# Order of the first loads: one whole x chunk on SP, the first wk piece and the gate vector first on ACT's queue

## The chip, the cores and the metric

The kernel runs on one core of a Trainium2 chip. A core has five engines that run beside one another: TensorE (PE, matrix products; PEld is its loading of stationary operands), VectorE (DVE), ScalarE (ACT), GpSimd (POOL) and SyncE (SP). Data comes from HBM by DMA. In this kernel DMAs are issued from SP and from ACT, each with a queue of its own, and run on the core's 16 DMA engines. The metric is the device time of one execution in microseconds; less is better.

## The reference, cut to what matters

```python
x = A_x                                              # 2048 rows x 640, bf16
g = _sigmoid((x * gate_w).sum(-1, keepdims=True))    # gate_w: 640 values
a = _A_ref(x, A_wqkv, A_wo)    # linear attention, 32 heads of 20: phi(q) (phi(k)^T v) / den, then @ wo
b = _B_ref(x, B_w1, B_w2, B_w3, B_w4)   # gelu(LN(x) @ w1), shifted rows, @ w2, + x; then an MLP 640-1728-640
return g * a + (1 - g) * b
# phi(t) = (t + 1 where t > 0, else exp(t)) + 1e-6
```

The first thing that the kernel computes is `phi(x @ wk)`, where `wk` is the middle third of `wqkv`, and with it the gate's logit `x @ gate_w`.

## The kernel before, in words

The 2048 rows are 16 chunks of 128 (`NCH`); the 640 columns are 5 pieces of 128 (`DC`). TensorE needs x with its columns on the partitions, so there is a tile `xT` of 5 pieces by 2048 rows. The order of instructions on each engine is the order of the code (a manual schedule).

Loads. `x_sb` chunk 0 comes as two halves of 64 rows, one first on SP's queue and one first on ACT's (L126, L127). Then come the five pieces of `wk` (`load_wk`, L124): piece 1 and 3 on SP, 0, 2 and 4 on ACT. The gate vector (`g5`, five rows of 128 values, 1.2 KB, L130) is third on ACT, behind wk piece 0. Then SP issues seven transposing DMAs that load chunks 1 to 15 straight into `xT` (`load_xT`, L121), and the loads of all later stages, among them wq (L136) and the other x chunks (`load_x`, L118). A DMA gets one of eight completion semaphores in turn, so the issue of a later one waits until the DMA that last used its semaphore has landed: before, the second transposing DMA waits for an x half, the third for wk piece 0, the fourth for wk piece 1, the fifth for the gate vector.

The opening on TensorE. `warmup(n, w)` (L201 to L203) issues `n` products of constants, `w` columns wide, whose results nobody reads. The program opens with `warmup(6)` (512 columns) and `warmup(3, P)` (128 columns) on L205 and L206. Then chunk 0 is transposed on TensorE in two turns (L212): pieces 0 and 1, then 2 to 4; VectorE copies each turn into `xT` (L213). Between the turns the gate vector is transposed (L215), and VectorE copies it into a further column of `wk_sb` (L216), so that the second product of each wk piece also gives the logit. Three more narrow fillers follow (L217; the first of them waits for that copy, since it writes the same PSUM tile).

Then the k stage (`k_mm`, L191): for each chunk and each piece two products, of 320 and 321 columns. In chunk 0 one filler of 256 columns stands behind each of the first four pieces (L221). ACT copies the logit of each finished chunk (`ylog`, L195) and takes the exponential (L183), VectorE makes `phi` from it. After 16 chunks come the q products (L233), and all later stages follow on TensorE without a pause: kv (L308), w1 (L342), w2 (L414), attention (L445), w3 (L461) and w4 (L480).

Of the kernel before, what the change touches and what calls it, by code (L numbers as in the profile page):

```python
# [16 lines left out]
def kernel(  # L17
# [14 lines left out]
    P = 128  # L32
    S, D = A_x.shape[1], A_x.shape[2]
# [21 lines left out]
    x2 = A_x.rearrange("b s d -> (b s) d")  # L55
# [13 lines left out]
    def pair():  # L69
        return ps.tile([P, 2, 512], F32, name="pp")  # L70


    x_sb = const.tile([P, NCH, D + 2], BF16)
# [41 lines left out]
    sp, aq, gq = nc.sync, nc.scalar, nc.gpsimd  # L115

    def load_x(c0, c1):
        sp.dma_start(x_sb[:, c0:c1, 0:D], x2[c0 * P:c1 * P, :].rearrange("(c p) d -> p c d", p=P))  # L118
# [4 lines left out]
    def load_wk(q, dc):  # L123
        q.dma_start(wk_sb[:, dc, 0:D], A_wqkv[dc * P:(dc + 1) * P, D:2 * D])  # L124

    for q, r0 in ((sp, 0), (aq, P // 2)):  # L126
        q.dma_start(x_sb[r0:r0 + P // 2, 0, 0:D], x2[r0:r0 + P // 2, :])  # L127
    load_wk(sp, 1)
    load_wk(aq, 0)
    aq.dma_start(g5[:], gate_w.rearrange("(c p) -> c p", p=P))  # L130
    load_wk(aq, 2)
    load_wk(sp, 3)
# [68 lines left out]
    def warmup(n, w=TS):  # L201
        for i in range(n):
            nc.tensor.matmul(warm[:, 1, 0:w], lhsT=one[:, 0:P], rhs=one[:, 0:w], start=True, stop=True)  # L203

    warmup(6)  # L205
    warmup(3, P)  # L206
    kp = pair()
    turns = [(pair()[:, 0, :].bitcast(BF16), a, b) for a, b in ((0, 2), (2, DC))]
    tg = warm[:, 0, :].bitcast(BF16)
# [387 lines left out]
```

## Time and profile before

| what | us |
|---|---|
| median of 3 runs | 270.51 |
| the runs | 270.07, 270.51, 271.04 |
| the profiled execution (the third of these) | 271.04 |
| its span on the core | 269.3 |
| TensorE busy | 262.1 |
| start of the first product (a filler) | 0.83 |
| start of the gate vector's transpose | 6.76 |
| start of the first k product | 7.49 |
| end of the k stage | 32.42 |

Times inside an execution are counted from the start of the span. A line of the timeline gives the start, the duration, the engine, the line of the kernel, the operation, what it writes and reads, and in brackets the idle time of the engine ahead of it with what ended that. A small q behind an engine's name is its queue, which issues DMAs and waits. A line of the waits has who waited for whom, then the total, the number of times and the longest. A line of DMA issues ends with the median time from issue to landing.

### The profile page before, as it was taken

How to read it: one execution, taken by the hardware profiler on the slowest of the kernel's cores; microseconds unless marked ns; L12 is line 12 of the kernel's file. 1: busy time of each engine (PE TensorE's matmuls, PEld its weight loads, DVE VectorE, ACT ScalarE, POOL GpSimd, SP SyncE). 2: the span in 40 equal slices, each digit the busy share in tenths (PEclk: the TensorE clock that was granted, in tenths of full speed). 3: DMA queues.
4: the chain of work that ended last, by engine and by line, in shares of the span. 5: the costliest groups of instructions: out<-in, count | busy, mean ns of one | idle time of the engine just before them, and what ended most of it. 6: DMA issues, size and time to landing. Idle time of an engine off the chain costs nothing.

```text
span 269.3 us, 4258 instructions
## 1 busy us (share of the span) xinstructions
PE 262.1 (97%) x1744; PEld 163.6 (61%) x1744; DVE 139.4 (52%) x270; ACT 85.1 (32%) x126; POOL 20.1 (7%) x55
## 2 busy tenths in 40 slices
PE   4999999999999999999999999999999999999994
PEld 1677655588855564565576555576555576555763
DVE  0278868799967498866323256233256233112132
ACT  1155544421244815831322131332131332142100
POOL 7100010002320032001000000100000100000000
PEclk9999999999999999999999999999999999999999
DMA  6999988004657524900041100041100041100011
GB/s 146 187 194 361 373 261 323 0 7 88 124 108 91 77 49 80 332 6 0 2 97 51 49 0 2 0 95 53 49 0 2 0 96 54 49 0 2 0 49 49
DMA packets 46108, 23.61 MB, mean 88 GB/s; under 512 B 35466, under 2 KB 45450, under 8 KB 46090
## 3 DMA queue, kind: packets, MB, share of 16 engines
q1 hardware_dynamic: 45568, 22.78, 32.9%
q10 hardware_dynamic: 522, 0.57, 1.2%
q8 instruction: 13, 0.21, 0.3%
q14 instruction: 5, 0.04, 0.1%
HBM read 12.21 MB, written 2.62 MB: 55 GB/s over the span
## 4 chain that ended last, share of the span: by engine, by line
PE 95%; DMA 2%; ACT 1%; ACTq 1%; DVE 0%; issue 0%
PE pp L480 21%; PE pp L461 21%; PE pp L191 9%; PE pp L308 8%; PE pp L414 8%; PE pp L445 8%; PE pp L342 8%; PE pp L233 8%; DMA g<-in_gate_w_dram 2%; PE pp L469 1%; PE pp L489 1%; ACT m_sb L382 1%; PE pp L361 1%; PE pp L248 0%; PE pp L203 0%; ACTq L124 0%
## 5 line engine op out<-in xcount | busy, mean ns | idle before, releaser
L461 PE MATMUL pp<-lnxT,w_sb 128*128 128x512 bf16 x260 | 60.4, 379 | 0.0
L480 PE MATMUL pp<-w_sb,h 128*128 128x256 bf16 (+1 forms) x416 | 57.9, 299 | 0.0
L463 ACT ACTIVATE h<-pp 128x1024 bf16<-128x1024 f32 (+1 forms) x28 | 26.9, 961 | 82.2 <-PE pp L461 82.2
L480 PEld LDWEIGHTS <-h 128*128 128x128 bf16 x416 | 40.3, 98 | 16.6 <-issue 1.1
L461 PEld LDWEIGHTS <-w_sb 128*128 128x128 bf16 x260 | 25.4, 98 | 26.8
L496 DVE SCALAR_TENSOR_TENSOR oc<-pp,omg,x 128x640 bf16<-128x640 f32 x15 | 12.9, 882 | 44.0 <-ACT h2x L472 21.3
L448 DVE SCALAR_TENSOR_TENSOR x<-pp,gate,x 128x640 f32<-128x640 f32 x16 | 13.9, 867 | 29.4 <-PE pp L445 29.4
L191 PE MATMUL pp<-wk_sb,xT 128*128 128x320 bf16 (+1 forms) x160 | 24.9, 317 | 0.0
L417 DVE TENSOR_TENSOR x<-pp,x_sb 128x640 f32<-128x640 f32 x16 | 13.1, 820 | 22.6 <-PE pp L414 22.6
L183 ACT ACTIVATE e<-pp 128x640 bf16<-128x640 f32 (+1 forms) x26 | 21.5, 826 | 9.6 <-PE pp L233 9.6
L445 PE MATMUL pp<-m_sb,pqT 128*128 128x320 bf16 x160 | 24.3, 299 | 0.0
L414 PE MATMUL pp<-w_sb,hsT 128*128 128x320 bf16 x160 | 23.9, 299 | 0.1
L308 PE MATMUL pp<-x_sb,pk 128*128 128x320 bf16 (+1 forms) x160 | 22.3, 300 | 0.0
L233 PE MATMUL pp<-xT,hsT 128*128 128x512 bf16 x100 | 21.7, 379 | 0.0
L308 PEld LDWEIGHTS <-pk 128*128 128x128 bf16 x160 | 18.8, 117 | 3.5
L191 PEld LDWEIGHTS <-xT 128*128 128x128 bf16 x160 | 16.5, 104 | 7.1
L414 PEld LDWEIGHTS <-hsT 128*128 128x128 bf16 x160 | 15.6, 98 | 8.2 <-issue 0.2
L445 PEld LDWEIGHTS <-pqT 128*128 128x128 bf16 x160 | 15.7, 98 | 7.7
L342 PE MATMUL pp<-lnxT,w_sb 128*128 128x512 bf16 x80 | 17.9, 379 | 0.0
L233 PEld LDWEIGHTS <-hsT 128*128 128x128 bf16 x100 | 11.8, 118 | 9.7
L278 POOL TENSOR_SCALAR rstd<-mv 128x4 f32<-128x4 f32 (+1 forms) x11 | 3.4, 312 | 160.1 <-DVE mv L284 160.1
L184 DVE TENSOR_SCALAR e<-e 128x640 bf16<-128x640 bf16 (+1 forms) x26 | 9.5, 365 | 10.5 <-ACT e L183 9.0
(77 smaller groups left out, 196.4 us busy)
## 6 DMA issues: line engine op xcount, KB each, us to landing
out_dram<-oc SPq DMA_DIRECT2D x15, 160.0 KB, 1.8
w_sb<-in_B_w_dram SPq DMA_DIRECT2D x1, 2160.0 KB, 8.5
w_sb<-in_B_w_dram SPq DMA_DIRECT2D x1, 2080.0 KB, 10.0
x_sb<-in_A_x_dram SPq DMA_DIRECT2D x2, 640.0 KB, 9.4
x_sb<-in_A_x_dram SPq DMA_DIRECT2D x1, 1120.0 KB, 8.1
wo_sb<-in_A_wo_dram SPq DMA_DIRECT2D x6, 160.0 KB, 7.4
hsT<-in_A_wqkv_dram SPq DMA_DIRECT2D x1, 800.0 KB, 5.6
m_sb<-in_A_wqkv_dram SPq DMA_DIRECT2D x1, 800.0 KB, 11.1
```

Source lines behind the costliest of these rows:

```text
L183: nc.scalar.activation(ev, src, ACT.Exp)
L191: nc.tensor.matmul(pt[:, hf, 0:n], lhsT=xT[:, dc, c * P:(c + 1) * P], rhs=wk_sb[:, dc, hf * HD:hf * HD + n], start=(dc == 0), stop=(dc == ...
L233: nc.tensor.matmul(pt[:, t % 2, :], lhsT=wq_sb[:, dc, :].rearrange("p (m j) -> p j m", j=DC)[:, j], rhs=xT[:, dc, t * TS:(t + 1) * TS], st ...
L308: nc.tensor.matmul(pt[:, hf, 0:HD + hf], lhsT=w, rhs=x_sb[:, c, hf * HD:(hf + 1) * HD + hf], start=(c == 0), stop=(c == NCH - 1))
L342: nc.tensor.matmul(pt[:, i, :], lhsT=w, rhs=lnxT[t][:, dc, :], start=(dc == 0), stop=(dc == DC - 1))
L414: nc.tensor.matmul(pt[:, hf, 0:HD], lhsT=hsT[:, fc, 2 + c * P:2 + (c + 1) * P], rhs=w2_sb[:, fc, hf * HD:(hf + 1) * HD], start=(fc == 0), ...
L417: nc.vector.tensor_tensor(x1[:].rearrange("p (h e) -> p h e", h=2), pt[:, :, 0:HD], x_sb[:, c, 0:D].rearrange("p (h e) -> p h e", h=2), op ...
L445: nc.tensor.matmul(pt[:, hf, 0:HD], lhsT=pqT[:, j, c * P:(c + 1) * P], rhs=m_sb[:, j, hf * HD:(hf + 1) * HD], start=(j == 0), stop=(j == D ...
L448: nc.vector.scalar_tensor_tensor(x1, pt[:, :, 0:HD], gate[:, c:c + 1], x1, op0=ALU.mult, op1=ALU.add)
L461: nc.tensor.matmul(pt[:, k, :], lhsT=w3_sb[:, dc, fc * P:(fc + 1) * P], rhs=lnT[:, dc, :], start=(dc == 0), stop=(dc == DC - 1))
L463: nc.scalar.activation(h2[:, 2 * i * TS:(2 * i + n) * TS], pt[:].rearrange("p h e -> p (h e)")[:, 0:n * TS], ACT.Gelu_apprx_tanh)
L480: nc.tensor.matmul(dst, lhsT=st[t]["h2"][:, fc * TS + cc * P:fc * TS + (cc + 1) * P], rhs=w4_sb[:, fc, a:b], start=start and fc == 0, stop ...
```

## The change

The first x chunk is loaded by one DMA on SP's queue. On ACT's queue wk piece 0 is now first and the gate vector second; pieces 2 and 4 follow as before. SP still issues wk pieces 1 and 3 second and third. There is one DMA less in all, so the semaphores are handed out differently: the second transposing DMA now waits for wk piece 0, the third for the x chunk, the fourth for the gate vector, the fifth for wk piece 1. In the opening of TensorE there are seven wide fillers and one narrow, in place of six and three. Nothing else differs; the lines below move up by one.

```diff
-    for q, r0 in ((sp, 0), (aq, P // 2)):
-        q.dma_start(x_sb[r0:r0 + P // 2, 0, 0:D], x2[r0:r0 + P // 2, :])
+    load_x(0, 1)
+    load_wk(aq, 0)
     load_wk(sp, 1)
-    load_wk(aq, 0)
     aq.dma_start(g5[:], gate_w.rearrange("(c p) -> c p", p=P))
     load_wk(aq, 2)
     load_wk(sp, 3)
     load_wk(aq, 4)
...
-    warmup(6)
-    warmup(3, P)
+    warmup(7)
+    warmup(1, P)
```

## The prediction

> **What bounds the kernel now.** I read the page first, then the waits and the chain of the opening, its timeline, and the DMA landings.
>
> The page: the profiled execution took 271.04 us, its span is 269.3, so 1.7 lie around the span. It is the slowest of the three runs, 0.53 above the median of 270.51. "Within 0.3%" below means within 0.81 us of that median.
>
> ```profile
> span 269.3 us, 4258 instructions
> PE 262.1 (97%) x1744; PEld 163.6 (61%) x1744; DVE 139.4 (52%) x270; ACT 85.1 (32%) x126; POOL 20.1 (7%) x55
> ```
>
> TensorE is busy for 97% of the span. The waits of the first 14 us and the waits of TensorE from there on say where the rest is:
>
> ```profile
> PE pp L215 <- DMA g<-in_gate_w_dram: 2.7, 1, 2.7
> PE pp L203 <- PEq L581: 0.8, 1, 0.8
> ```
>
> Apart from its first instruction, TensorE waits once in the whole program, 2.7 us for the 1.2 KB gate vector. After it the products follow one another to the end. So what starts that stream earlier shortens the kernel by as much, unless another wait comes in. The opening in order of time (ACT's queue and TensorE):
>
> ```profile
> 0.79 0.56 ACTq L127 DMA_DIRECT2D x_sb<-in_A_x_dram  x1
> 0.83 3.04 PE L203 MATMUL pp<-const-bfloat16-1.0 128*128 128x512 bf16 x9 [0.83 <-PEq L581]
> 1.39 0.86 ACTq L124 DMA_DIRECT2D wk_sb<-in_A_wqkv_dram  x1
> 2.27 0.58 ACTq L130 DMA_DIRECT2D g<-in_gate_w_dram  x1
> ...
> 3.66 0.42 PE L212 MATMUL pp<-ident,x_sb 128*128 128x128 bf16 x2
> 6.76 0.18 PE L215 MATMUL pp<-ident,g 5*128 5x5 bf16 x1 [2.68 <-DMA g<-in_gate_w_dram]
> ...
> 7.49 0.74 PE L191 MATMUL pp<-wk_sb,xT 128*128 128x320 bf16 x2
> ```
>
> The gate vector is issued third on ACT's queue, at 2.27, and lands 4.4 later, at 6.7. The pace comes next. The chain gives 0.53 for a pair of L191 products, while chunk 0 is worked; ACT's copy of each finished chunk's gate logit shows the pace behind it:
>
> ```profile
> 7.69 0.53 PE pp L191 x2
> ```
> ```profile
> 11.26 0.16 ACT L195 COPY ylog<-pp 128x1 f32<-128x1 f32 x1 [6.09 <-PE pp L191]
> 13.38 0.16 ACT L195 COPY ylog<-pp 128x1 f32<-128x1 f32 x1 [1.36 <-PE pp L191]
> 14.74 0.16 ACT L195 COPY ylog<-pp 128x1 f32<-128x1 f32 x1 [0.60 <-PE pp L191]
> ```
>
> Chunk 1 takes 2.12, chunk 2 and all later ones 1.36, half of 5 x 0.53. TensorE goes over to the double pace inside chunk 1, at (2.12-1.36)/(2.65-1.36) = 59% of its slow products: 11.02 (where chunk 1 begins) + 1.56, about 12.6. That is 5.9 us after its last idle ended at 6.76. The 3.0 us of fillers from 0.83, ended by the wait, were not enough for it. (The granted clock reads full throughout; the pace is what I go by.)
>
> Last, the DMA views of 2.0 to 4.1 us, then of 4.1 to 6.7 (q1 is SP's queue, q10 ACT's; packets, MB, share), and the DMAs issued near 3.0 with their time to landing:
>
> ```profile
> DMA packets 482, 0.54 MB, mean 259 GB/s; under 512 B 58, under 2 KB 482, under 8 KB 482
> q10 hardware_dynamic: 203, 0.23, 36.8%
> ```
> ```profile
> DMA packets 812, 0.43 MB, mean 166 GB/s; under 512 B 582, under 2 KB 812, under 8 KB 812
> q10 hardware_dynamic: 183, 0.20, 55.3%
> q1 hardware_dynamic: 629, 0.23, 48.7%
> ```
> ```profile
> wk_sb<-in_A_wqkv_dram ACTq DMA_DIRECT2D x1, 160.0 KB, 5.6
> xT<-in_A_x_dram SPq DMA_TRANSPOSE x1, 6.6
> ```
>
> From 4.1 on the packets are small ones of the transposing DMAs, and less is moved.
>
> **The change part by part.**
>
> *Fillers.* Before x's turn 6 wide and 3 narrow products become 7 and 1. The weight loads of wide ones start 0.43 apart, three narrow ones take 0.32: +0.43 - 0.21 = 0.22. The first x transpose moves from 3.66 to 3.88. Today this hides in the 2.68 of wait for the vector; if that cover is gone it costs 0.22.
>
> *First x chunk in one DMA on SP.* The halves land 2.3 and 2.6 after 0.79, at 3.1 and 3.4. The whole chunk is 80 KB more on SP's queue, while the first wk piece now runs beside it from ACT. Bounds: 3.1 (SP's half) and 4.2 (SP's second DMA, issued at 1.40, landing 2.8 later, after 240 KB). I take the middle, 3.7, ahead of the fillers' end; the upper bound costs 0.3. SP still issues three DMAs before its first transposing DMA (2.49), so those keep their times; POOL's queue issues none. The third transposing DMA waits on the semaphore of wk piece 0 for 0.7 now (SP's waits); the order after gives it x's semaphore, and the second gets that of piece 0.
>
> The Trainium skill, "DMA: Bandwidth & Descriptors", Queues, rings and completion order, says that each DMA engine goes round between the queues that have work, packet by packet; this speaks against the change, since x then shares the engines with wk piece 0, where its halves shared them with each other only. By that rule x lands with 320 KB moved instead of 160; the rows' bound of 4.2 has 240 KB moved on SP alone and about as much beside it, so rule and bound ask for no other sum.
>
> *Gate vector.* One issue of 0.56 goes from in front of it: issued near 1.7. Ahead of it on ACT's queue stand 160 KB, not 240. Queue 10 (ACT's) moves 0.23 MB in 2.0 to 4.1, which is all that stood ahead of the vector; at this 0.11 MB/us 160 KB take 1.5, so its turn comes near 3.6 instead of 4.1. It landed 2.6 after its turn, in that second stretch of 166 GB/s. Bounds: 3.6 + 0.3 = 3.9 (the two x halves landed 0.3 apart) and 3.6 + 2.6 = 6.2. I take 4.2, because its turn now lies in the stretch in which x and wk piece 1 landed without such a delay. Then the first k product comes 0.73 later (6.76 to 7.49 today), at 4.9 for 7.49. VectorE's copies of x's transposes (0.29, 0.36) end before they are needed.
>
> *What is late next.* The five wk pieces are needed 0.75 apart (L191 pair and filler): 4.9, 5.7, 6.4, 7.2, 7.9. Before, pieces 0, 1 and 3 landed at 5.8, 4.2, 7.1; 0 is now first on its queue, so in time. Pieces 2 and 4 landed at 2.88 + 5.6 = 8.5 and 9.0, and the second x chunk (2.49 + 6.6) at 9.1. Pieces 2 and 4 have 80 KB less ahead of them. Queue 10 moves 0.20 MB in 4.1 to 6.7, so they gain between 0 and 1.05: piece 2 lands between 7.4 and 8.5. I take 7.5: the queue is never empty in that stretch, so less ahead shows nearly in full. From it chunk 0 has 2 x 0.75 + 0.53 at the slow pace: chunk 1 starts at 9.5; at the fast pace it waits for its x at 9.1. Bounds for chunk 1's start: 9.1 and 10.5, before 11.02.
>
> *Pace.* TensorE now works without a hole from 0.83 to 6.4: 5.6 us, where 5.9 preceded the change of pace. If that is enough, chunk 1 runs at 1.36 and its extra 0.76 goes too; if the pace changes at 12.6 as before, half of what is won in the start is lost again.
>
> The Trainium skill, "TensorE: Matmul & The Clock Gate", Part 1, has the clock released after a busy window of about 3.4 us, free-running. By it the opening's 5.6 us hold a whole window in (5.6-3.4)/3.4, about 6 of 10 phases; the trace's one change of pace fits such a window and does not prove it.
>
> *Sum.* Chunk 1 starts at 9.4 instead of 11.02: -1.62. No slow products in it: -0.76. Together -2.38: 271.04 - 2.4 = **268.7**. I make no deduction for the profiled run's 0.53 above the median: I estimate that this is when the pace changes, and in this case all of chunk 1 is fast. Later stages take it: x chunks 8 to 11 land at 10.69 + 6.9 = 17.6 and are then needed at 9.4 + 7 x 1.36 = 18.9.
>
> **The rivals.**
>
> *B, early start, old pace.* The vector lands in time, but the waits for wk piece 2 break the run and the pace changes near 12.6. Won: (11.02 - 9.5)/2 = 0.76: 270.3. For it: 5.6 is under 5.9. Against: the run is near that length.
>
> *C, the vector still late.* It keeps its 2.6 of delay and lands at 6.2 instead of 6.7. Half of 0.6 is won at the old pace: 270.7. For it: its delay has nothing to do with its size. Against: its turn comes before the transposing DMAs.
>
> *D, slower: the second x chunk becomes the wait.* SP's queue holds 80 KB more ahead of its transposing DMA. Queue 1 moves 0.23 MB in 4.1 to 6.7, so 80 KB can cost 0.9: it lands at 10.0 and TensorE idles until then. If the 5.9 us to the fast pace count from there, the slow stretch costs 5.9/2 = 2.95 instead of 0.76: (10.0 - 11.02) + 2.95 - 0.76 = +1.2: 272.2. It decides for slower (over 271.3) from a landing of 9.1 on, with TensorE still slow by then. For it: it landed at 9.1 before. Against: ACT's queue, which shares the engines, has 80 KB less.
>
> **How the numbers follow.** A 0.45, B 0.22, C 0.13, D 0.20. A's own range is 267.9 (chunk 1 at 8.9) to 269.5 (at 10.2). Without D the range is 267.9 to 271.3. Faster: nearly all of A and a quarter of B (270.3 less the spread of 0.5) = 0.50; the same: the rest of B and C = 0.28; slower: D and a little of C = 0.22.
>
> **What would show it.** L215 near 4.2 with an idle under 0.3 before it (over 1.5: C). First L191 near 4.9; idle of TensorE before the third pair, put down to a wk piece on ACT's queue; chunk 1 from 9.4. The first two logit copies 1.36 apart, for A; about 2.6 for B and D. TensorE waiting on xT past 9.1 would be D. The step likeliest to fail is the pace, then piece 2's landing.

## The result, and the profile after

The changed kernel takes 266.87 us (median of 4 runs, 266.47 to 266.91) against 270.76 for the kernel before on the same chip (4 runs): a ratio of 0.9857, with a 95% interval of 0.9834 to 0.9879. It is faster by 3.9 us. The prediction had 268.7 with a range of 267.9 to 271.3, so the direction is right and the time lies 1.0 us below the range.

The page of the profiled execution after (266.86 us):

```profile
span 265.2 us, 4253 instructions
PE 260.5 (98%) x1743; PEld 162.8 (61%) x1743; DVE 139.3 (53%) x270; ACT 85.1 (32%) x126; POOL 20.3 (8%) x55
```

The waits of the first 14 us, and ACT's queue and TensorE in order of time. All kernel lines have a number one lower than before: L190 are the k products, L211 the transposes of x, L214 that of the gate vector.

```profile
PE pp L202 <- PEq L580: 0.8, 1, 0.8
PEld L211 <- DMA x_sb<-in_A_x_dram: 0.3, 1, 0.3
```
```profile
0.79 0.40 ACTq L124 DMA_DIRECT2D wk_sb<-in_A_wqkv_dram  x1
1.22 0.59 ACTq L129 DMA_DIRECT2D g<-in_gate_w_dram  x1
1.85 0.84 ACTq L124 DMA_DIRECT2D wk_sb<-in_A_wqkv_dram  x2
```
```profile
3.88 0.42 PE L211 MATMUL pp<-ident,x_sb 128*128 128x128 bf16 x2
4.23 0.18 PE L214 MATMUL pp<-ident,g 5*128 5x5 bf16 x1
...
5.04 0.74 PE L190 MATMUL pp<-wk_sb,xT 128*128 128x320 bf16 x2
5.57 0.42 PE L202 MATMUL pp<-const-bfloat16-1.0 128*128 128x256 bf16 x1
5.79 0.74 PE L190 MATMUL pp<-wk_sb,xT 128*128 128x320 bf16 x2
6.32 0.34 PE L202 MATMUL pp<-const-bfloat16-1.0 128*128 128x256 bf16 x1
6.50 0.44 PE L190 MATMUL pp<-wk_sb,xT 128*128 128x320 bf16 x2
...
7.26 6.98 PE L190 MATMUL pp<-wk_sb,xT 128*128 128x320 bf16 x50
```

The vector's transpose starts at 4.23 instead of 6.76, and no wait takes its place: from 3.88 on TensorE does not wait. The k products go from 0.74 for a pair to 0.44 between 5.79 and 6.50, so the fast pace is there within chunk 0. ACT's logit copies show the same:

```profile
7.73 0.16 ACT L194 COPY ylog<-pp 128x1 f32<-128x1 f32 x1 [3.73 <-PE pp L190]
9.09 0.16 ACT L194 COPY ylog<-pp 128x1 f32<-128x1 f32 x1 [0.60 <-PE pp L190]
```

The k stage ends at 28.13 instead of 32.42, 4.29 earlier. The first k product comes 2.45 earlier (7.49 to 5.04), chunk 0 takes 2.49 instead of 3.53 (1.04), and chunk 1 takes 1.36 instead of 2.16 (0.80). The rest of the program is as long as before: TensorE's last product ends 233.3 after the k stage in both. The three parts make 4.29 together.

What the prediction did not have is the loads. Here is the DMA view of 4.1 to 6.7 after, then the issues near 2.2 (after; wk piece 4 and the second x chunk), with the time to landing:

```profile
DMA packets 1191, 0.59 MB, mean 226 GB/s; under 512 B 896, under 2 KB 1191, under 8 KB 1191
...
q1 hardware_dynamic: 923, 0.29, 67.8%
q10 hardware_dynamic: 268, 0.30, 39.7%
```
```profile
wk_sb<-in_A_wqkv_dram ACTq DMA_DIRECT2D x1, 160.0 KB, 4.5
xT<-in_A_x_dram SPq DMA_TRANSPOSE x1, 5.1
```

In the same stretch as before 226 GB/s are moved instead of 166. ACT's queue, which moves wk pieces there, needs less of the engines for more bytes: 268 packets for 39.7% of 16 engines over 2.6 us are 62 ns a packet, where 183 for 55.3% were 126 ns. So the loads on ACT's queue and the second x chunk land 1.8 to 2.5 us earlier (the vector by its transpose; times in us from the start of the span). On SP's queue wk piece 1 lands at 4.1 as before, piece 3 at 6.1 for 7.1, and the first x chunk a little later, at 3.6 for 3.1 and 3.4:

| run | wk 0 | vector's transpose | wk 2 | wk 4 | second x chunk | chunk 1 starts |
|---|---|---|---|---|---|---|
| before | 5.8 | 6.76 | 8.5 | 9.0 | 9.1 | 11.02 |
| after | 3.8 | 4.23 | 6.3 | 6.7 | 7.3 | 7.53 |

### The profile page after: what moved, and what is told of

It reads as the page before. It is cut to its first block, busy times and chain, and to the rows that moved or that the text cites. A ratio compares the mean times of both kernels' runs of the same rounds, so it can differ in the third digit from the quotient of the medians.

```text
span 265.2 us, 4253 instructions
## 1 busy us (share of the span) xinstructions
PE 260.5 (98%) x1743; PEld 162.8 (61%) x1743; DVE 139.3 (53%) x270; ACT 85.1 (32%) x126; POOL 20.3 (8%) x55
## 4 chain that ended last, share of the span: by engine, by line
PE 97%; ACT 1%; DVE 0%; issue 0%
PE pp L479 22%; PE pp L460 21%; PE pp L190 8%; PE pp L307 8%; PE pp L413 8%; PE pp L444 8%; PE pp L341 8%; PE pp L232 8%; PE pp L202 2%; PE pp L468 1%; PE pp L488 1%; ACT m_sb L381 1%; PE pp L360 1%; PE pp L247 0%; PE pp L379 0%; PE pp L211 0%
## 5 line engine op out<-in xcount | busy, mean ns | idle before, releaser
L479 PEld LDWEIGHTS <-h 128*128 128x128 bf16 x416 | 40.3, 98 | 16.6 <-issue 1.1
L190 PE MATMUL pp<-wk_sb,xT 128*128 128x320 bf16 (+1 forms) x160 | 23.1, 304 | 0.0
L190 PEld LDWEIGHTS <-xT 128*128 128x128 bf16 x160 | 15.9, 99 | 6.2
L184 DVE SCALAR_TENSOR_TENSOR pk<-pp,e 128x640 bf16<-128x640 f32 x16 | 13.2, 825 | 1.7
```

Of the source, the lines that this page charges most:

```text
L184: nc.vector.scalar_tensor_tensor(dst, src, 0.0, ev, op0=ALU.max, op1=ALU.add)
L190: nc.tensor.matmul(pt[:, hf, 0:n], lhsT=xT[:, dc, c * P:(c + 1) * P], rhs=wk_sb[:, dc, hf * HD:hf * HD + n], start=(dc == 0), stop=(dc == ...
L479: nc.tensor.matmul(dst, lhsT=st[t]["h2"][:, fc * TS + cc * P:fc * TS + (cc + 1) * P], rhs=w4_sb[:, fc, a:b], start=start and fc == 0, stop ...
```

## The experiments

The theory after the result: the gate vector's wait was one of two things that held TensorE back, and the order of the loads moved the wk pieces too. The rivals: the vector alone carries the gain, or the longer run of fillers does.

### The two parts apart

e1_fillers_only, against before:

```diff
-    warmup(6)
-    warmup(3, P)
+    warmup(7)
+    warmup(1, P)
```

> Loads as before, only the opening fillers are 7 wide and 1 narrow. Theory 1 (the order of the loads carries the whole gain): the gate vector lands near 6.7, TensorE's wait for it shrinks from 2.68 to about 2.46, and the time stays at 270.8 within 0.5. Theory 2 (the longer run of fillers brings the fast pace forward, and with it the gain): the pace changes before 9 and the time comes to 267 to 269.

Measured: 270.31 us (269.53 to 271.08), ratio 0.9995, interval 0.9965 to 1.0026. The wait for the vector is still there, 0.26 shorter, about what the fillers are longer:

```profile
6.71 0.18 PE L215 MATMUL pp<-ident,g 5*128 5x5 bf16 x1 [2.42 <-DMA g<-in_gate_w_dram]
```

e2_loads_only, against after:

```diff
-    warmup(7)
-    warmup(1, P)
+    warmup(6)
+    warmup(3, P)
```

> Loads as after, opening fillers 6 wide and 3 narrow as before. Theory 1: x (landed at 3.60 after) and the gate vector (3.73) are there in time, the first k product comes at 4.9 to 5.1, and the time is 266.9, at most 0.2 less. Theory 2: the pace changes later, 268 or more.

Measured: 267.16 us (266.77 to 267.27), ratio 0.9889, interval 0.9831 to 0.9946. In its profiled execution x landed at 3.85, so the transposes started at 3.90 in spite of the shorter fillers; the pace was fast from 4.0 on, and TensorE then waited 0.7 for wk piece 2. The gain is that of the loads; the theory of the fillers falls.

### The vector alone

e3_halves_g_second, against before:

```diff
+    aq.dma_start(g5[:], gate_w.rearrange("(c p) -> c p", p=P))
     load_wk(sp, 1)
     load_wk(aq, 0)
-    aq.dma_start(g5[:], gate_w.rearrange("(c p) -> c p", p=P))
```

> Before with one move: the gate vector goes ahead of wk piece 0 on ACT's queue, the x halves and the fillers stay. The vector lands before 4 and TensorE no longer waits for it. Theory 1a (wk pieces 2 and 4 and the second x chunk land near 8.5, 9.0 and 9.1 in any order that has an x half ahead of wk piece 0 on ACT's queue): chunk 1 starts at 9.1 to 10.5 and the time is near 268.7, as the prediction had it. Theory 1b (the gate vector's place is all): chunk 1 starts near 7.5 and the time is 266.9.

Measured: 270.15 us (268.31 to 272.09), ratio 1.0002, interval 0.9962 to 1.0041. TensorE:

```profile
4.04 0.18 PE L215 MATMUL pp<-ident,g 5*128 5x5 bf16 x1
4.15 0.50 PE L212 MATMUL pp<-ident,x_sb 128*128 128x128 bf16 x3
4.55 0.36 PE L203 MATMUL pp<-const-bfloat16-1.0 128*128 128x128 bf16 x3
6.45 0.43 PE L191 MATMUL pp<-wk_sb,xT 128*128 128x320 bf16 x2 [1.54 <-DMA wk_sb<-in_A_wqkv_dram]
...
8.30 0.69 PE L191 MATMUL pp<-wk_sb,xT 128*128 128x320 bf16 x2 [0.93 <-DMA wk_sb<-in_A_wqkv_dram]
```

The vector is there at 4.04, as early as after, and nothing is won. Two waits take the place of the one: for wk piece 0, which lands at 6.4, and for piece 2, which lands at 8.3. Chunk 1 starts at 10.28. There is a second cost. These are stretches of TensorE: busy time and instructions of PE and PEld, further engines, then the granted clock:

```profile
4.64:8.04 3.40, 1.19 (x10) 0.73 (x9) 0.36 (x1) 0.54 (x1) 2.47 (x9) 1.00 1.09 165
8.06:11.40 3.34, 3.10 (x13) 1.81 (x13) 0.08 (x1) 0.77 (x2) 0.00 (x0) 0.50 1.06 204
11.50:15.00 3.50, 3.50 (x28) 2.50 (x27) 2.45 (x5) 1.53 (x4) 0.00 (x0) 1.00 1.08 185
```

The fast pace had come at 4.6 (the first pair takes 0.43). In the next 3.4 us TensorE was busy for 1.19 only, and the clock went back to a half for another 3.4 (the pair at 8.30 takes 0.69). "TensorE: Matmul & The Clock Gate" of the Trainium skill, Part 1, has the clock decided in free-running windows of 3413 ns; the records of this run agree, with 3.413 us granted and 3.413 taken back. Theory 1a had the landings right (8.3, 8.8 and 8.8 for pieces 2, 4 and the second x chunk) and chunk 1 within its bounds, but its 268.7 has neither the clock that is taken back nor the wait for piece 0.

e4_no_gate_wait, against before:

```diff
-            nc.tensor.transpose(tg[:, 0:DC], g5[:], ident[0:DC, 0:DC])
-            nc.vector.tensor_copy(wk_sb[:, :, D], tg[:, 0:DC])
+            nc.vector.tensor_copy(wk_sb[:, :, D], ident[:, 0:DC])
```

> Loads and their order exactly as before; the transpose of the gate vector is left out, and the logit column of wk gets five columns of the identity instead, so the gate is computed from a wrong vector. TensorE then never waits for the vector. It shows what is late next in the loads of before. Theory 1a: TensorE waits for wk piece 2 until about 8.5, chunk 1 starts at 9.1 to 10.5, 268.7. Theory 1b: no wait takes the vector's place, chunk 1 starts near 7.3, and the time is 266.7.

The kernel leaves out the transpose of the vector; the column for the logit gets columns of the identity. Measured: 270.24 us (267.69 to 271.73), ratio 0.9972, interval 0.9934 to 1.0011. The waits of its profile:

```profile
5.94 0.43 PE L191 MATMUL pp<-wk_sb,xT 128*128 128x320 bf16 x2 [1.52 <-DMA wk_sb<-in_A_wqkv_dram]
...
8.89 0.69 PE L191 MATMUL pp<-wk_sb,xT 128*128 128x320 bf16 x2 [2.03 <-DMA wk_sb<-in_A_wqkv_dram]
```

With the loads as before and no wait for the vector at all, TensorE waits 3.5 us for wk pieces 0 and 2, and the time is that of before. In the kernel before, the 2.7 us of wait for the vector were therefore worth next to nothing by themselves.

### The vector late, the wk pieces early

e11_g_last, against after:

```diff
-    aq.dma_start(g5[:], gate_w.rearrange("(c p) -> c p", p=P))
     load_wk(aq, 2)
     load_wk(sp, 3)
     load_wk(aq, 4)
+    aq.dma_start(g5[:], gate_w.rearrange("(c p) -> c p", p=P))
```

> After with the gate vector last on ACT's queue, behind wk piece 4. It is issued near 2.7 and lands behind piece 4, at 6.4 to 7; the wk pieces land as after or a little earlier. Theory 7 (early wk pieces and an early vector are both needed, and the later of the two sets TensorE's start): TensorE waits some 2.5 us as before, the pace changes at 10 to 13.5, chunk 1 starts at 10 to 11, time 269.5 to 270.5. Theory 8 (the wk pieces alone carry the gain): 267.5 or less.

Measured: 269.61 us (267.98 to 270.98), ratio 0.9975, interval 0.9948 to 1.0001.

```profile
6.52 0.18 PE L214 MATMUL pp<-ident,g 5*128 5x5 bf16 x1 [2.22 <-DMA g<-in_gate_w_dram]
```

Pieces 0, 2 and 4 land at 4.0, 4.8 and 6.1, and TensorE waits for the vector until 6.52; chunk 1 starts at 10.27. So early wk pieces alone gain at most half a per cent, an early vector alone gains nothing that these runs can tell (e3: 1.0002, from 0.9962 to 1.0041), and both together gain 1.4%: two loads were late by about as much, and the later of the two sets the start.

### Why the wk pieces land earlier

Two things differ ahead of them on ACT's queue: 80 KB of x, and the time that the issues take, 1.0 us by wk piece 2 (issued at 2.88 before, 1.85 after). Behind both stands the question why pieces 2 and 4 then need 5.6 us from issue to landing.

e5_whole_g_first, against after (or e3_halves_g_second with the x chunk whole, and with the fillers of after):

```diff
+    aq.dma_start(g5[:], gate_w.rearrange("(c p) -> c p", p=P))
     load_wk(aq, 0)
     load_wk(sp, 1)
-    aq.dma_start(g5[:], gate_w.rearrange("(c p) -> c p", p=P))
```

> After with the gate vector ahead of wk piece 0 on ACT's queue: the whole x chunk stays on SP, so this is the run with the vector first and halved x, with the halves undone. Theory 1c (80 KB of x and its 0.56 us issue ahead of wk piece 0 on ACT's queue are what made all wk pieces late): wk piece 0 lands by 4.6, piece 2 by 6.7, the second x chunk by 7.7, time 266.9 within 0.4. Theory 1d (whatever stands ahead of wk piece 0 makes it late, by the later issue): piece 0 lands past 5.5, piece 2 past 8, time near 270.

Measured: 266.35 us (266.31 to 266.43), ratio 0.9861, interval 0.9841 to 0.988. Pieces 0, 2 and 4 land at 4.5, 5.8 and 6.2, the second x chunk at 6.8, and chunk 1 starts at 6.85. Against e3_halves_g_second the halves are undone (the fillers too, which e1 and e2 showed to matter little), and the 3.8 us are back. "DMA: Bandwidth & Descriptors" of the Trainium skill, Rules for kernel authors, advises one 128-partition transfer over two to disjoint partition halves, since both use the same engines; these two runs agree with the advice. They don't show that its reason is the one at work here: the half also makes ACT issue wk piece 0 later (2.42 in e3, 1.39 in e5), and the next runs look at that.

e6_plain_x, against before:

```diff
     def load_xT(c0, c1):
-        sp.dma_start_transpose(xT[:, :, c0 * P:c1 * P], x2[c0 * P:c1 * P, :])
+        for c in range(c0, c1):
+            sp.dma_start(xT[:, :, c * P:(c + 1) * P], x2[c * P:(c + 1) * P, :].rearrange("p (c s) -> p c s", c=DC))
```

> Before with the transposing DMAs of x chunks 1 to 15 put as plain DMAs of the same bytes, one for each chunk, in runs of 256 bytes: x isn't transposed, so k and q are of wrong numbers. The loads ahead of them keep order and issue times. Theory 3 (wk pieces 0, 2 and 4 were late because they shared the DMA engines with transposing DMAs): pieces 2 and 4 land before 7 though issued as before, the gate vector before 5.5. Theory 4 (they were late because they are issued late and have 80 KB more ahead): 8.5 and 9.0 as before, within 0.5.

Here x reaches the k products untransposed. Measured, one run: 268.40 us. Pieces 0, 2 and 4 land at 4.8, 7.3 and 8.0, the vector is transposed at 5.23. That is between the two theories: 1.0 to 1.2 us less than before. But with the loads of before piece 2 landed at 7.9 (e1), 8.5 and 8.9 (e4), so the size of this is uncertain. The DMA view of 4.1 to 6.7 says more:

```profile
DMA packets 1288, 0.66 MB, mean 253 GB/s; under 512 B 953, under 2 KB 1288, under 8 KB 1288
q1 hardware_dynamic: 1012, 0.35, 54.5%
q10 hardware_dynamic: 276, 0.31, 40.3%
```

SP's queue moves more beside ACT's than before (0.35 MB for 0.23), and still a packet of ACT's takes 61 ns (40.3% of 16 engines over 2.6 us for 276), not 126.

e7_hold_transposes, against before (`hold` is a scratch tile):

```diff
     load_wk(aq, 4)
+    sp.dma_start(hold[:], wk_sb[0:16, 4, 0:P])
```

> Before with one small DMA on SP ahead of the first transposing one, which copies 16 x 256 bytes of wk piece 4 to a scratch tile; so no transposing DMA is issued until piece 4 has landed. Theory 3: with no transposing DMA beside them wk pieces 0, 2 and 4 land by 4.6, 5.5 and 6.2, the gate vector by 4.7, and the second x chunk near 9.5 to 10 (issued some 4 us later); TensorE then waits for that chunk, time 269 to 271. Theory 4: pieces 2 and 4 land at 8 or later all the same, and the time is 272 or more.

Measured, one run: 271.21 us. The DMA issue of wk piece 2 in this run, then the stretch of 4.1 to 6.7:

```profile
wk_sb<-in_A_wqkv_dram ACTq DMA_DIRECT2D x1, 160.0 KB, 3.6
```
```profile
DMA packets 431, 0.48 MB, mean 185 GB/s; under 512 B 56, under 2 KB 431, under 8 KB 431
...
q10 hardware_dynamic: 304, 0.34, 42.1%
q1 hardware_dynamic: 127, 0.14, 14.9%
```

Halves, queue order and bytes ahead are those of before; pieces 0, 2 and 4 land at 4.7, 6.2 and 6.7 all the same, and the vector is transposed at 4.70. Pieces 2 and 4 were issued 0.2 and 0.4 earlier than before (2.65 and 3.03), but landed 2.3 earlier: 3.6 after their issue instead of 5.6. A packet of ACT's queue takes 58 ns (42.1% of 16 engines over 2.6 us for 304). So it was the transposing DMAs that made the vector and the wk pieces late in the order of before; plain DMAs in their place (e6) delayed the landing by less. The kernel is not faster for it, since the second x chunk now lands at 10.25 and TensorE waits for that.

e9_act_late, against e5_whole_g_first:

```diff
+    for n in (D, D, D, HD):
+        nc.gpsimd.memset(wk_sb[:, 2, 0:n], 0.0)
     load_wk(aq, 2)
```

> The order of the run with whole x and the vector first, but wk piece 2 is issued only when four writes of GpSimd to its tile are done (near 2.9, as before, instead of 1.78), and piece 4 after it (near 3.4 instead of 2.25); the results are the reference's. The bytes on each queue stay as in that run. Theory 5 (the later issue on ACT is what lets the transposing DMAs overtake pieces 2 and 4): they land at 7.5 to 9 instead of 5.8 and 6.2. Theory 6 (the 80 KB of x on ACT's queue are what does it): at most 0.7 later than in that run, 6.5 and 6.9.

Measured, one run: 268.53 us. Pieces 2 and 4 were issued at 3.25 and 3.62 and landed at 8.2 and 9.4, with every byte on the queue where e5 has it:

```profile
8.23 0.43 PE L192 MATMUL pp<-wk_sb,xT 128*128 128x320 bf16 x2 [2.57 <-DMA wk_sb<-in_A_wqkv_dram]
```
```profile
DMA packets 1035, 0.39 MB, mean 152 GB/s; under 512 B 895, under 2 KB 1035, under 8 KB 1035
...
q1 hardware_dynamic: 905, 0.24, 63.4%
q10 hardware_dynamic: 130, 0.15, 46.9%
```

1.4 us later at the issue become 2.4 to 3.2 later at the landing, and the stretch is back at 152 GB/s, 150 ns for a packet of ACT's queue. The issues came 0.4 and 0.2 later than in the kernel before (2.88 and 3.40), the landings near its 8.5 and 9.0. So the later issue alone brings the lateness back; the 80 KB are not needed for it.

e10_xT_early, against after:

```diff
+    load_xT(1, 2)
     load_wk(sp, 3)
     load_wk(aq, 4)
-    for c0, c1 in ((1, 2), (2, 3), (3, 4), (4, 6), (6, 8), (8, 12), (12, 16)):
+    for c0, c1 in ((2, 3), (3, 4), (4, 6), (6, 8), (8, 12), (12, 16)):
```

> After with the first transposing DMA (x chunk 1) ahead of wk piece 3 on SP's queue, so that transposing begins some 0.6 us earlier, with all issues on ACT as after. Theory 3 (transposing beside wk pieces is what makes them late): pieces 2 and 4 land 1 to 2 us later than after (6.3 and 6.7), piece 3 too, and TensorE waits for one of them. Otherwise they land as after within 0.4, and only piece 3 comes later.

Measured, one run: 268.38 us. Pieces 2 and 4 are issued as after (1.84 and 2.24). Piece 2 lands at 6.1 (6.3 after), piece 4 at 8.0 (6.7 after). Piece 3 lands at 8.4 (6.1 after), and TensorE waits 1.53 for it; but behind the moved DMA it was also issued 1.3 later, at 3.05, so it tells little. Even the second x chunk, issued 0.47 earlier, lands later: 8.2 for 7.3. The expectation holds for piece 4, not for piece 2. For piece 4 the cause put back brings the effect back.

What makes the difference is the order, and not only that transposing packets run beside. This is 4.7 to 6.7 in the kernel after:

```profile
DMA packets 1078, 0.46 MB, mean 231 GB/s; under 512 B 881, under 2 KB 1078, under 8 KB 1078
q1 hardware_dynamic: 892, 0.26, 80.2%
q10 hardware_dynamic: 186, 0.21, 31.2%
```

The transposing DMAs are at work there too, and a packet of ACT's queue takes 54 ns (31.2% of 16 engines over 2.0 us for 186). But all runs with transposing DMAs fall into two groups. Where pieces 2 and 4 were issued at most 0.13 after the first transposing DMA, they landed 3.5 to 4.6 after their issue (after, e2, e5, e8, e11, piece 2 of e10). Where they were issued 0.3 or more after it, they took 4.9 to 6.0 (before, e1, e3, e4, e9, piece 4 of e10). In e6, with plain DMAs in that place, they took 4.4 and 4.5 although issued 0.4 and 1.0 after the first of these. For the small vector 0.2 ahead was not enough: before, it was issued at 2.27 and landed 4.4 later. Why the order decides is not shown.

The landings of all these runs in one table (us from the start of the span; the last column is the median, or the one run):

| run | wk 0 | vector's transpose | wk 2 | wk 4 | second x chunk | chunk 1 starts | us |
|---|---|---|---|---|---|---|---|
| e3, vector alone early | 6.4 | 4.04 | 8.3 | 8.8 | 8.8 | 10.28 | 270.15 |
| e4, no wait for it | 5.9 | none | 8.9 | 9.6 | 9.5 | 10.87 | 270.24 |
| e11, vector late | 4.0 | 6.52 | 4.8 | 6.1 | 6.7 | 10.27 | 269.61 |
| e5, whole x, vector first | 4.5 | 4.14 | 5.8 | 6.2 | 6.8 | 6.85 | 266.35 |
| e7, transposing held | 4.7 | 4.70 | 6.2 | 6.7 | 10.3 | 10.30 | 271.21 |
| e9, ACT issues late | 4.5 | 4.02 | 8.2 | 9.4 | 8.3 | 9.69 | 268.53 |
| e10, transposing early | 3.9 | 4.22 | 6.1 | 8.0 | 8.2 | 9.05 | 268.38 |

### The fillers, and the two orders side by side

e8_no_fillers, against after:

```diff
-    warmup(7)
-    warmup(1, P)
```

> After without the opening fillers: TensorE starts with the transposes of x, at 3.6 to 3.9. Theory A (the pace of TensorE changes only after an unbroken run of 5 to 6 us or a whole window of 3.4 us, so the fillers are worth the slow products that they take on themselves): the pace changes at 7 to 10.5 instead of 6.4, chunk 0 and much of chunk 1 are slow, time 267.5 to 269.5. Rival (the fillers are worth nothing): 266.9 within 0.3.

Measured: 267.84 us (267.59 to 268.36), ratio 0.9922, interval 0.9894 to 0.9949; e5_whole_g_first on the same chip took 266.35. TensorE starts at 3.76, all of chunk 0 runs at the slow pace, and the pace changes at 8.1; chunk 1 starts at 8.28. The opening fillers are worth 0.7 to 1.5 us here, by bringing the fast pace forward: 1.5 against e5, which has the other order; 1.0 against the 266.87 of after, taken on another chip; 0.7 between the two profiled executions (267.59 and 266.86), where chunk 1 starts at 8.28 instead of 7.53.

after_again and e5_again are the kernel after and e5_whole_g_first once more, on one chip.

> After once more, on one chip with the next run. 0.986 of before within 0.003, median 266.9.

> Whole x on SP, gate vector first and wk piece 0 second on ACT. In its first run chunk 1 started at 6.85 against 7.53 after, so it should be 0.3 to 0.7 us under after on the same chip. If that was chance, both come within 0.2.

Measured: after 266.78 us (266.48 to 267.15), ratio 0.9889, interval 0.9871 to 0.9907; the other order 266.5 us (266.21 to 267.02), ratio 0.9881, interval 0.9865 to 0.9898. The medians lie 0.28 us apart and the ranges overlap: if the vector-first order is better, it is by 0.1%, which these runs don't settle.

The profile of after_again shows what bounds the kernel now. In it the fast pace comes earlier than in the first profile of after, before the first k product:

```profile
4.86 0.43 PE L190 MATMUL pp<-wk_sb,xT 128*128 128x320 bf16 x2
6.41 0.43 PE L190 MATMUL pp<-wk_sb,xT 128*128 128x320 bf16 x2 [0.62 <-DMA wk_sb<-in_A_wqkv_dram]
```

TensorE then waits for wk piece 2, which lands at 6.4, chunk 1 starts at 7.44 instead of 7.53, and the time is the same (266.78 and 266.86). So a still earlier pace gains next to nothing: what it saves is waited for piece 2.

## Why the prediction was right or wrong

- *What bounds the kernel now.* TensorE's only wait was read rightly, and the sentence that an earlier start of the stream shortens the kernel "unless another wait comes in" holds; but what was behind that wait was put too small. e4_no_gate_wait shows 3.5 us of wait for wk pieces 0 and 2 right behind it.
- *Fillers.* Right: the first x transpose at 3.88, as worked out.
- *First x chunk.* x landed at 3.6 (taken 3.7, bounds 3.1 and 4.2): right. The rule weighed there, that x then shares the engines with wk piece 0, is borne out as far as x lands later than the halves did (3.1 and 3.4), and it cost nothing, since the fillers cover it. In e5_whole_g_first, where piece 0 is issued 0.6 later (1.39), x landed at 3.1.
- *Gate vector.* Landed at 3.7 (taken 4.2, bounds 3.9 and 6.2), transposed at 4.23, first k product at 5.04 (4.9): the place and the reason were right, the time a little too late. Its issue came at 1.22, not near 1.7: the step took away the 0.56 of the half's issue, but the issue of wk piece 0 also shrank, from 0.86 to 0.40. That the vector's delay belongs to the stretch in which it lands, the reason given, is what e7_hold_transposes shows directly: with no transposing DMA beside it the vector's transpose starts at 4.70 even in the order of before.
- *What is late next.* This is the step that failed. It gave chunk 1's start bounds of 9.1 and 10.5 and took 9.4; it measured 7.53. Piece 2 was given 7.5 with a lower bound of 7.4 and landed at 6.3, and the second x chunk was held at 9.1 and landed at 7.3. The step took the 0.20 MB that ACT's queue moved in 4.1 to 6.7 as the rate of that stretch and only moved bytes along it. But the rate belonged to the order of before and its transposing DMAs: 126 ns a packet (before), 58 with these held back (e7), 62 after. Pieces 2 and 4 were issued 1.0 and 1.2 us earlier (1.85 and 2.23 for 2.88 and 3.40), about as early as the first transposing DMA (2.18) or ahead of it, where before they came 0.4 and 0.9 behind it (2.49); e9_act_late takes the early issue away and gets 8.2 and 9.4 back. The second x chunk was also issued 0.3 earlier, since SP's issues did not keep their times: the whole chunk took 0.40, the half 0.56. Piece 0 was dismissed with "in time", which held after, but in the order of before it stood right behind the vector, with 1.5 us of wait of its own (e3, e4).
- *Pace.* Right in its result: chunk 1 ran at 1.36. But the 5.9 us that were weighed there are not what the change of pace needs: in after_again it came before 4.86, at most 4.0 us after the first filler. A part was missed: the pace changed within chunk 0. The step let a fast chunk 0 end at the landing of the second x chunk, 9.1. With the loads of after and a slow chunk 0, e8_no_fillers starts chunk 1 at 8.28; so of the 1.87 between 9.4 and 7.53 some 1.1 are the landings, and 0.75 the pace in chunk 0.
- *Sum.* -2.38 was forecast for the profiled execution, -4.18 measured. The start of chunk 1 gave -3.49 instead of -1.62; chunk 1 itself gave -0.80, as put (-0.76).
- *The rivals.* None came. B's mechanism, waits that break the run and take the fast pace back, is what e3_halves_g_second shows. C and D did not happen: the second x chunk lands earlier, although SP's queue has 80 KB more ahead of it. The range's lower end of 267.9 rested on the same held x chunk and was too high by 1.0. By the sum's own terms chunk 1 at 8.9 would have given 268.2 (271.04 - 2.12 - 0.76), so the end was not even the one that was worked out.

## What to carry to other kernels

When one wait ends last, work out what stands right behind it by its own landing time, and try the kernel with that wait left out before counting on it: here leaving it out gained nothing, and two loads had to move together. A transfer's time to landing is not a rate that can be moved along with its bytes; look which other transfers ran beside it, and issue what is needed first well ahead of the transposing DMAs in time, on every queue. And a hole in TensorE's opening costs twice, once as the wait and once as the slow pace that follows.

## What was not expected of the hardware

- Transposing DMAs on SP's queue can more than double the time of a packet on ACT's: 126 and 150 ns (before, e9), 58 with them held back (e7), 61 with plain DMAs of the same bytes in 256-byte runs in their place (e6). It takes the order for that: after, with them beside, it was 54 in 4.7 to 6.7. Which resource they share was not tried and stays open.
- A DMA issue takes the queue's time unevenly: 0.40 for the first one of 160 KB after, 0.56 for a half of 80 KB, 0.60 and 0.86 for the wk piece behind that half (e7, before), 0.56 to 0.99 for the 1.2 KB of the gate vector. On ACT this added up to 1.0 us between the two orders at wk piece 2.
- The clock is taken back as well as granted, in steps of 3.41 us. A window with TensorE busy for 1.19 of 3.40 (e3) lost it; e9_act_late kept it with 1.92 and 1.91 of 3.4 us. The profile reads full clock also where the pace shows a half (before, up to 12.6), so only a lower figure tells something.
- The runs of the orders with a hole in the opening spread widely: 267.77 to 271.68 for before beside the first four runs, 268.31 to 272.09 for e3, against 266.47 to 267.15 for after in both its turns. It would fit windows that start at another point of each run; that was not tested by itself.
